# One transfer for x's first two contraction blocks, all TensorE transposes ahead of the first product, and the table load ahead of gate rows

## The chip, the cores and the metric

The kernel runs on one core of a Trainium2 chip. The metric is the device time of one execution in microseconds (us); the times before are 273.25 us in the median of three runs, from 272.84 to 273.96.

## The reference

A feed-forward block with a gated GELU, in bf16, with 1024 tokens (32 x 32), a model width of 1024 and an inner width of 3584:

```python
def reference(x, w_gate, w_up, w_down):
    return (_gelu(x @ w_gate) * (x @ w_up)) @ w_down
```

`x` is (32, 32, 1024), `w_gate` and `w_up` are (1024, 3584), `w_down` is (3584, 1024). `_gelu` is the tanh approximation.

## The kernel before

The tokens are split into two halves of 512 and the contraction of 1024 into eight blocks of 128. The kernel replaces plain 2 x 2 block products by a scheme with fewer products: it forms sums and differences of quarters of the weights (`s1` to `s4`) and of x (`t1` to `t4`) and multiplies those. x is kept transposed, with the contraction on the partitions, in four tiles: `b11` and `b12` hold contraction blocks 0 to 3 for the two token halves, `b21` and `b22` blocks 4 to 7.

The first stage is called ahead in the code. It multiplies the lower half of the gate weights by `b21`, for 24 output tiles in six groups of four (`i` is the group, `j` the tile in it, `k` one of four contraction blocks). The weights of group `i` are in `a12_ahead[i]`, filled by `load_ahead(i, k0, k1)` (L204 to L209); `product_ahead` (L288 to L297) issues the matmuls of some `k` and some columns. This stage starts as soon as the first pieces of x and of the weights have arrived, and this start is all that the change touches.

How the start is arranged, in an order written out by hand (`manual_schedule`):

- The constants and the identity `ident` are made by GpSimd (POOL). TensorE (PE) runs `NWARM` = 6 matmuls on constants (L254), which compute nothing that is used.
- Contraction blocks 4 and 5 of x for the first token half arrive untransposed in `x_nat`, one transfer of 128 KB each: block `dt` = 0 on the queue of SyncE (SP), block `dt` = 1 on the queue of ScalarE (ACT). They are called the first and the second x block below. Each has rows of 256 bytes. Block pieces are transposed by TensorE (L266, four per block), written to PSUM tiles `tps`, and copied to `b21[:, dt]` by VectorE (DVE) in two halves of 256 tokens (L271).
- Contraction blocks 6 and 7 come by a transposing transfer (`load_xT(0, KD + KQ, DT)`, L222) on SP's queue. A tiny GpSimd copy (L221), which reads `x_nat` and writes into the same destination, makes it wait until the first x block has landed.
- Gate weights of groups 0 and 1: SP issues group 0 `k` = 0, group 1 `k` = 0, group 0 `k` = 2 and 3 in one transfer; after the transposing transfer it issues group 1 `k` = 2 and 3. ACT issues, behind a small probe load and the second x block, `k` = 1 of groups 0 and 1. After these five issues, ACT runs a one-column GELU on `ident` (L250 through the helper at L246), ahead of which its table is loaded.
- TensorE's order is: warm matmuls; four transposes of the first x block; `NFILL` = 7 further matmuls on constants, 128 columns each (L275); `by_halves(0)`, that is group 0, `k` = 0, 256 tokens at a time, eight matmuls; four transposes of the second x block; group 1, `k` = 0, for three of four tiles; `by_halves(1)`; the rest of group 1, `k` = 0 and 1; then `k` = 2 and 3 of both groups, each tile copied out when it is complete (L348). Groups 2 to 5 follow.

For the first x block the two token halves have a PSUM tile of their own each; for the second they share one (`whole_tp`). PSUM tiles with the tag A rotate through six banks, so one of group 1's tiles takes over the bank of `whole_tp`; hence its late place in the order.

Of the kernel before, what the change touches and what calls it, by code (L numbers as in the profile page):

```python
# [8 lines left out]
ACT = mybir.ActivationFunctionType  # L9
# [4 lines left out]
def kernel(  # L14
# [20 lines left out]
    nc = tc.nc  # L35
    P = nc.NUM_PARTITIONS
    fp32 = mybir.dt.float32
    f32r = mybir.dt.float32r
    bf16 = mybir.dt.bfloat16
# [3 lines left out]
    xf = x.flatten_outer_dims()  # L43
# [6 lines left out]
    KD = DT // 2  # L50
# [4 lines left out]
    KQ = DT // 4  # L55
    HF = FT // 2
    MT = NB // P
    NWARM = 6
    NFILL = 7
    KB = 4  # L60
    QF = HF // 2
    batches = [(0, KB), (KB, QF), (QF, QF + KB), (QF + KB, HF)]
# [13 lines left out]
    ps1 = ctx.enter_context(tc.tile_pool(name="ps1", bufs=2, space=bass.MemoryType.PSUM))  # L76
# [29 lines left out]
    BANKS = {"A": 6, "C": 2}  # L106

    def acc(tag):
        return ps1.tile([P, NB], fp32, name=f"ps{tag}", tag=tag, bufs=BANKS[tag])
# [3 lines left out]
    a12_ahead = [ring.tile([P, KD, KB * P], bf16, name="a12a", tag="ring") for _ in range(2)]  # L113
    b11 = xpool.tile([P, KD, NB], bf16, name="b11")
    b21 = xpool.tile([P, KD, NB], bf16, name="b21")
# [66 lines left out]
    ones_w = nc.const_aps.tensor(1.0, [P, P], bf16)  # L182
    ones_m = nc.const_aps.tensor(1.0, [P, NB], bf16)
    ident = xpool.tile([P, P], bf16, name="ident")
    make_identity(nc, ident)
    NB_P = NB // P
    probe = xpool.tile([P // 4, KD, 2], bf16, name="probe")
    HALF = NB_P // 2
    x_nat = spool.tile([P, NB_P, KQ * P], bf16, name="x_nat", tag="s1")

    with tc.manual_schedule():
        def load_nat(eng, dt, p0, p1):
            eng.dma_start(
                out=x_nat[:, p0:p1, dt * P : (dt + 1) * P],
                in_=xf[p0 * P : p1 * P, (KD + dt) * P : (KD + dt + 1) * P].rearrange("(b p) d -> p b d", p=P),
            )

        assert KQ == 2
        load_nat(nc.sync, 0, 0, NB_P)


        nc.scalar.dma_start(out=probe, in_=wg_r[::4, KD:, :2])

        def load_ahead(i, k0, k1, eng=nc.sync, j0=0, j1=KB):  # L204
            f0 = i * KB
            eng.dma_start(
                out=a12_ahead[i][:, k0:k1, j0 * P : j1 * P],
                in_=wg_r[:, KD + k0 : KD + k1, (f0 + j0) * P : (f0 + j1) * P],
            )  # L209

        def load_xT(nb, d0, d1):
            t = ((b11, b12), (b21, b22))[d0 // KD][nb]
            nc.sync.dma_start_transpose(
                out=t[:, d0 % KD : (d1 - 1) % KD + 1, :], in_=xf[nb * NB : (nb + 1) * NB, d0 * P : d1 * P]
            )

        load_ahead(0, 0, 1)
        load_nat(nc.scalar, 1, 0, NB_P)
        load_ahead(1, 0, 1)
        load_ahead(0, KQ, KD)  # L220
        nc.gpsimd.tensor_copy(b21[:1, KQ, :1], x_nat[:1, 0, :1])  # L221
        load_xT(0, KD + KQ, DT)  # L222
        load_ahead(0, 1, KQ, nc.scalar)
        load_ahead(1, 1, KQ, nc.scalar)
        a12_ahead += [spool.tile([P, KD, KB * P], bf16, name="a12b", tag=t) for t in ("s2", "s4", "s1", "s3")]
        load_ahead(1, KQ, KD)
        def load_halves(i):
# [16 lines left out]
        def gelu(src, tag, bufs):  # L244
            h = ework.tile([P, NB], bf16, name=tag, tag=tag, bufs=bufs)[:, : src.shape[-1]]
            nc.scalar.activation(h, src, ACT.Gelu_apprx_tanh)  # L246
            return h


        gelu(ident[:, :1], "h0", 6)  # L250

        warm_ps = acc("A")
        for _ in range(NWARM):
            nc.tensor.matmul(warm_ps, lhsT=ones_w, rhs=ones_m, start=True, stop=True)  # L254

        def tp_tile(cols):
            return ps1.tile([P, cols], bf16, name="tp", tag="A", bufs=BANKS["A"])

        tps = [[tp_tile(HALF * P) for _ in range(2)]]
        whole_tp = tp_tile(NB_P * P)  # L260
        tps.append([whole_tp[:, h * HALF * P : (h + 1) * HALF * P] for h in range(2)])

        def transposed(dt):
            for half, tp in enumerate(tps[dt]):
                for b in range(HALF):
                    nc.tensor.transpose(  # L266
                        tp[:, b * P : (b + 1) * P], x_nat[:, half * HALF + b, dt * P : (dt + 1) * P], ident
                    )
            for half, tp in enumerate(tps[dt]):
                p0 = half * HALF * P  # L270
                nc.vector.tensor_copy(b21[:, dt, p0 : p0 + HALF * P], tp)  # L271

        transposed(0)
        for _ in range(NFILL):
            nc.tensor.matmul(warm_ps[:, :P], lhsT=ones_w, rhs=ones_w, start=True, stop=True)  # L275

        def prod(ps, lhs, rhs, start):
            for k in range(KD):
# [9 lines left out]
        def product_ahead(ps, i, j, k0=0, k1=KD, cols=slice(None)):  # L288
            for k in range(k0, k1):
                nc.tensor.matmul(  # L290
                    ps[:, cols],
                    lhsT=a12_ahead[i][:, k, j * P : (j + 1) * P],
                    rhs=b21[:, k, cols],
                    start=(k == 0 and not cols.start),
                    stop=(k == KD - 1),
                    skip_group_check=True,
                )  # L297
# [32 lines left out]

        both = (nc.scalar.copy, nc.vector.tensor_copy)
        ps = [[acc(t) for t in tags] for tags in ("CCAA", "AAAA")]
        def by_halves(k):
            for half in range(2):
                for j in range(KB):
                    product_ahead(ps[0][j], 0, j, k, k + 1, slice(half * HALF * P, (half + 1) * HALF * P))

        by_halves(0)
        transposed(1)
        for j in range(KB - 1):  # L340
            product_ahead(ps[1][j], 1, j, 0, 1)
        by_halves(1)
        for j in range(KB):
            product_ahead(ps[1][j], 1, j, 0 if j == KB - 1 else 1, KQ)
        for i in (0, 1):
            for j in range(KB):
                product_ahead(ps[i][j], i, j, KQ)
# [26 lines left out]
        for ci in range(NCH):  # L374
# [8 lines left out]
            sn5, sn2, h1, h0 = [], [], [], []  # L383
# [17 lines left out]
            if fts[-1] < NAHEAD:  # L401
                h0 = first
# [192 lines left out]
        for h0, h1, upto in ((0, NB - P, NB - P), (NB - P, NB, NB)):  # L595
            cols = slice(h0, h1)
            ps = acc("C")[:, : h1 - h0]
# [33 lines left out]
```

## Time and profile before

| what | value |
|---|---|
| median of the runs | 273.25 us (272.84 to 273.96) |
| the profiled execution | 273.33 us |
| its span, first to last instruction | 271.4 us |
| TensorE busy | 268.0 us, 99% of the span, 1219 matmuls |
| VectorE / ScalarE / GpSimd busy | 75% / 43% / 45% |
| first product matmul starts | 4.46 us into the span |

The profiled time is 1.9 us more than the span; that is what lies around the first and last instruction. A busy TensorE in the profile is not a TensorE at its best pace, and the matmuls' ends are modelled: consecutive matmuls overlap in the record, so the pace is read from the distance between starts. In a timeline row the first number is the start in us, the second the time to the end of the last merged instruction, and `x4` says how many were merged. PE is TensorE's matmuls, PEld its weight loads, SPq and ACTq are instructions that issue transfers from SyncE and ScalarE.

### The profile page before, as it was taken

Reading aid. Unit: us, or ns where it says so; the run is one execution under the profiler, and the core shown is the slowest. Engines: PE = TensorE matmul, PEld = TensorE weight load, DVE = VectorE, ACT = ScalarE, POOL = GpSimd, SP = SyncE. Lnnn points to the kernel's source line nnn. Section 1 sums busy time; section 2 is a strip of 40 time slices with the busy share of each in tenths; the row PEclk is TensorE's granted clock in tenths of the full one; section 3 lists DMA queues with packets and bytes.
Section 4 is the critical chain, followed back from the end, with each engine's and each line's share of the span. In section 5 each row is a group of like instructions: output and inputs, shape, how many; then the busy total and the mean of one; then the engine's idle time right before and its main releaser. Section 6 shows DMA issues by size and latency. Waiting matters only on the chain.

```text
span 271.4 us, 3431 instructions
## 1 busy us (share of the span) xinstructions
PE 268.0 (99%) x1219; PEld 193.7 (71%) x1219; DVE 204.0 (75%) x205; ACT 115.4 (43%) x189; POOL 120.8 (45%) x61
## 2 busy tenths in 40 slices
PE   8999999999999999999999999999999999999996
PEld 5544776886787788688688687764458888888884
DVE  1447999986976877887777478469999999988711
ACT  2435756545644653645636535434000307870000
POOL 1080089997994994995995996000000000000000
PEclk9999999999999999999999999999999999999999
DMA  7999321514505505415234190005981537875111
GB/s 193 316 209 228 100 62 56 157 35 119 157 0 155 156 2 155 126 28 157 73 84 119 47 331 8 0 2 178 356 279 60 156 115 248 269 194 181 52 64 60
DMA packets 56657, 35.88 MB, mean 132 GB/s; under 512 B 10048, under 2 KB 56640, under 8 KB 56640
## 3 DMA queue, kind: packets, MB, share of 16 engines
q1 hardware_dynamic: 53232, 33.17, 43.3%
q10 hardware_dynamic: 3408, 2.49, 2.9%
q8 instruction: 10, 0.16, 0.3%
q14 instruction: 7, 0.06, 0.1%
HBM read 31.72 MB, written 2.10 MB: 125 GB/s over the span
## 4 chain that ended last, share of the span: by engine, by line
PE 99%; DVE 0%; issue 0%
PE psA L279 38%; PE psA L435 24%; PE psC L279 19%; PE psC L435 7%; PE psA L290 5%; PE psC L290 3%; PE psC L599 1%; PE psA L254 1%; PE psA L275 0%; PE tp L266 0%; DVE o_last L600 0%
## 5 line engine op out<-in xcount | busy, mean ns | idle before, releaser
L279 PE MATMUL psA<-t,s 128*128 128x512 f32 x224 | 57.2, 397 | 0.0
L246 ACT ACTIVATE h<-c 128x512 bf16<-128x512 f32 x56 | 34.4, 629 | 41.5 <-DVE c L309 41.5
L279 PEld LDWEIGHTS psA<-t,s 128*128 128x128 f32 x224 | 42.1, 188 | 9.5
L165 POOL TENSOR_TENSOR s<-wu 128x1024 fp32r<-128x1024 bf16 x13 | 29.5, 2271 | 28.0 <-DMA wu<-in_w_up_dram 24.0
L166 POOL TENSOR_TENSOR s<-s,wg 128x1024 fp32r<-128x1024 f32 x14 | 32.0, 2285 | 15.2 <-PE psA L279 14.2
L279 PE MATMUL psA<-b,wg 128*128 128x512 bf16 x128 | 29.4, 380 | 0.0
L168 POOL TENSOR_TENSOR s<-wg,wu 128x1024 fp32r<-128x1024 bf16 x13 | 28.9, 2219 | 0.0
L279 PE MATMUL psA<-t,a22r 128*128 128x512 f32 x112 | 27.9, 391 | 0.0
L279 PE MATMUL psC<-t,s 128*128 128x512 f32 x112 | 27.9, 391 | 0.0
L279 PE MATMUL psC<-b22r,s 128*128 128x512 f32 x112 | 27.7, 389 | 0.0
L309 DVE TENSOR_TENSOR c<-sn,psA 128x512 f32<-128x512 f32 x32 | 21.8, 682 | 6.7 <-PE psA L279 6.1
L314 ACT COPY sn<-psC 128x512 f32<-128x512 f32 x28 | 16.3, 588 | 22.8 <-PE psC L279 14.9
L279 PEld LDWEIGHTS psC<-t,s 128*128 128x128 f32 x112 | 21.0, 188 | 4.5
L279 PEld LDWEIGHTS psA<-t,a22r 128*128 128x128 f32 x112 | 21.0, 188 | 4.5
L279 PEld LDWEIGHTS psC<-b22r,s 128*128 128x128 f32 x112 | 21.0, 188 | 4.4
L309 DVE TENSOR_TENSOR c<-sn,psC 128x512 f32<-128x512 f32 x28 | 19.0, 686 | 6.0 <-PE psC L279 6.0
L412 DVE TENSOR_TENSOR lo<-c,h 128x512 bf16<-128x512 f32 x14 | 22.5, 1605 | 0.9
L279 PEld LDWEIGHTS <-wg 128*128 128x128 bf16 x128 | 11.8, 98 | 15.3 <-issue 2.4
L167 POOL TENSOR_TENSOR s<-wg,s 128x1024 fp32r<-128x1024 bf16 x10 | 21.6, 2160 | 0.8
L314 ACT COPY sn<-psA 128x512 f32<-128x512 f32 x32 | 18.3, 592 | 4.9 <-PE psA L279 4.6
L309 DVE TENSOR_TENSOR c<-ahead,psA 128x512 f32<-128x512 f32 x24 | 16.4, 686 | 3.5 <-PE psA L279 2.1
L412 DVE TENSOR_TENSOR hi<-c,h 128x512 bf16<-128x512 f32 x14 | 17.6, 1257 | 0.9
(88 smaller groups left out, 375.5 us busy)
## 6 DMA issues: line engine op xcount, KB each, us to landing
wu<-in_w_up_dram SPq DMA_DIRECT2D x14, 512.0 KB, 4.1
wdb<-in_w_down_dram SPq DMA_DIRECT2D x12, 512.0 KB, 4.8
wg<-in_w_gate_dram SPq DMA_DIRECT2D x10, 512.0 KB, 5.3
wdb<-in_w_down_dram SPq DMA_DIRECT2D x12, 384.0 KB, 4.5
v<-in_w_down_dram SPq DMA_DIRECT2D x4, 512.0 KB, 6.1
out_dram<-o_sb ACTq DMA_DIRECT2D x15, 128.0 KB, 1.7
v<-in_w_down_dram SPq DMA_DIRECT2D x4, 384.0 KB, 7.5
a12b<-in_w_gate_dram SPq DMA_DIRECT2D x4, 256.0 KB, 4.2
```

What stands on the lines that cost most here:

```text
L165: yield engs[0].tensor_tensor(s1, a21, a22, ADD)
L166: yield engs[1].tensor_tensor(s2, s1, a11, SUB)
L167: yield engs[2].tensor_tensor(s4, a12, s2, SUB)
L168: yield engs[3].tensor_tensor(s3, a11, a21, SUB)
L246: nc.scalar.activation(h, src, ACT.Gelu_apprx_tanh)
L254: nc.tensor.matmul(warm_ps, lhsT=ones_w, rhs=ones_m, start=True, stop=True)
L279: nc.tensor.matmul(ps, lhsT=lhs[:, k, :], rhs=rhs[:, k, :], start=(start and k == 0), stop=(k == KD - 1), skip_group_check=True,)
L290: nc.tensor.matmul(ps[:, cols], lhsT=a12_ahead[i][:, k, j * P : (j + 1) * P], rhs=b21[:, k, cols], start=(k == 0 and not cols.start), stop ...
L309: tt(t, s, ps, ADD)
L314: nc.scalar.copy(t, ps)
L412: tt(g_of(ft)[:, NB:], added(sn5[fl], psa[fl]), h1[fl], MUL)
L435: nc.tensor.matmul(banks[m], lhsT=lhs(k)[:, m * P : (m + 1) * P], rhs=rhs(k), start=(start and k == 0), stop=(k == HF - 1), skip_group_che ...
```

## The change

The two x blocks come in one transfer on SP's queue, with rows of 512 bytes. ACT's queue loses its x transfer; its one-column GELU moves up behind the probe, and now writes into the first column of group 1's `k` = 1 weights, which the transfer issued next overwrites. So ACT issues three gate transfers behind it: group 1 `k` = 1, then group 0 `k` = 2 and `k` = 3 one by one. Group 0 `k` = 1 moves to SP, ahead of the transposing transfer.

On TensorE the fillers become two ahead of the transposes and one behind. All eight transposes stand ahead of the first product, in the order block 0 half 0, block 0 half 1, block 1 half 0, block 1 half 1. The two PSUM tiles are now one per token half, each holding both blocks; four VectorE copies follow in the order of the transposes. The products then run group 0 `k` = 0 by halves, group 1 `k` = 0, group 0 `k` = 1 and group 1 `k` = 1 whole, and from there on as before.

```diff
-        load_nat(nc.sync, 0, 0, NB_P)
+        load_nat(nc.sync, 0, NB_P)
...
         load_ahead(0, 0, 1)
-        load_nat(nc.scalar, 1, 0, NB_P)
         load_ahead(1, 0, 1)
-        load_ahead(0, KQ, KD)
+        load_ahead(0, 1, KQ)
+        nc.scalar.activation(a12_ahead[1][:, 1, :1], ident[:, :1], ACT.Gelu_apprx_tanh)
+        load_ahead(1, 1, KQ, nc.scalar)
+        for k in range(KQ, KD):
+            load_ahead(0, k, k + 1, nc.scalar)
         nc.gpsimd.tensor_copy(b21[:1, KQ, :1], x_nat[:1, 0, :1])
         load_xT(0, KD + KQ, DT)
-        load_ahead(0, 1, KQ, nc.scalar)
-        load_ahead(1, 1, KQ, nc.scalar)
...
-        gelu(ident[:, :1], "h0", 6)
...
-        transposed(0)
-        for _ in range(NFILL):
-            nc.tensor.matmul(warm_ps[:, :P], lhsT=ones_w, rhs=ones_w, start=True, stop=True)
+        tps = [ps1.tile([P, KQ, HALF * P], bf16, name="tp", tag="A", bufs=BANKS["A"]) for _ in range(2)]
...
+        fill(2)
+        for dt in range(KQ):
+            for half in range(2):
+                transposed(half, dt)
+        for dt in range(KQ):
+            for half in range(2):
+                copied(half, dt)
+        fill(1)
...
-        by_halves(0)
-        transposed(1)
-        for j in range(KB - 1):
+        for half in range(2):
+            for j in range(KB):
+                product_ahead(ps[0][j], 0, j, 0, 1, slice(half * HALF * P, (half + 1) * HALF * P))
+        for j in range(KB):
             product_ahead(ps[1][j], 1, j, 0, 1)
-        by_halves(1)
-        for j in range(KB):
-            product_ahead(ps[1][j], 1, j, 0 if j == KB - 1 else 1, KQ)
+        for i in (0, 1):
+            for j in range(KB):
+                product_ahead(ps[i][j], i, j, 1, KQ)
```

More of the change, by code (lines that the diff above doesn't have):

```diff
@@ L58 @@
     NWARM = 6
-    NFILL = 7
     KB = 4
@@ L191, with load_nat @@
     with tc.manual_schedule():
-        def load_nat(eng, dt, p0, p1):
+        def load_nat(eng, p0, p1):
             eng.dma_start(
-                out=x_nat[:, p0:p1, dt * P : (dt + 1) * P],
-                in_=xf[p0 * P : p1 * P, (KD + dt) * P : (KD + dt + 1) * P].rearrange("(b p) d -> p b d", p=P),
+                out=x_nat[:, p0:p1, :],
+                in_=xf[p0 * P : p1 * P, KD * P : (KD + KQ) * P].rearrange("(b p) d -> p b d", p=P),
             )
         assert KQ == 2
-        load_nat(nc.sync, 0, 0, NB_P)
+        load_nat(nc.sync, 0, NB_P)
         nc.scalar.dma_start(out=probe, in_=wg_r[::4, KD:, :2])
@@ L254, with fill, transposed, copied @@
             nc.tensor.matmul(warm_ps, lhsT=ones_w, rhs=ones_m, start=True, stop=True)
[L256 to L271, printed above, removed]
-        transposed(0)
-        for _ in range(NFILL):
-            nc.tensor.matmul(warm_ps[:, :P], lhsT=ones_w, rhs=ones_w, start=True, stop=True)
+        def fill(n):
+            for _ in range(n):
+                nc.tensor.matmul(warm_ps[:, :P], lhsT=ones_w, rhs=ones_w, start=True, stop=True)
+        tps = [ps1.tile([P, KQ, HALF * P], bf16, name="tp", tag="A", bufs=BANKS["A"]) for _ in range(2)]
+        def transposed(half, dt):
+            for b in range(HALF):
+                nc.tensor.transpose(
+                    tps[half][:, dt, b * P : (b + 1) * P],
+                    x_nat[:, half * HALF + b, dt * P : (dt + 1) * P],
+                    ident,
+                )
+        def copied(half, dt):
+            p0 = half * HALF * P
+            nc.vector.tensor_copy(b21[:, dt, p0 : p0 + HALF * P], tps[half][:, dt, :])
+        fill(2)
[6 more added lines that the diff above has]
+        fill(1)
         def prod(ps, lhs, rhs, start):
@@ L332 @@
         ps = [[acc(t) for t in tags] for tags in ("CCAA", "AAAA")]
-        def by_halves(k):
-            for half in range(2):
-                for j in range(KB):
-                    product_ahead(ps[0][j], 0, j, k, k + 1, slice(half * HALF * P, (half + 1) * HALF * P))
-        by_halves(0)
-        transposed(1)
-        for j in range(KB - 1):
+        for half in range(2):
+            for j in range(KB):
+                product_ahead(ps[0][j], 0, j, 0, 1, slice(half * HALF * P, (half + 1) * HALF * P))
+        for j in range(KB):
             product_ahead(ps[1][j], 1, j, 0, 1)
-        by_halves(1)
-        for j in range(KB):
-            product_ahead(ps[1][j], 1, j, 0 if j == KB - 1 else 1, KQ)
+        for i in (0, 1):
+            for j in range(KB):
+                product_ahead(ps[i][j], i, j, 1, KQ)
         for i in (0, 1):
```

## The prediction

> **What bounds the kernel now.** I read first the chain of work that ended last.
>
> ```profile
> PE 99%; DVE 0%; issue 0%
> ```
>
> TensorE is the chain nearly from end to end, so an edit at the start is worth the time by which it moves TensorE's dense run of products, and nothing else. The waits of TensorE and of its weight loads over the first 60 us name one transfer:
>
> ```profile
> PEld L254 <- issue: 1.8, 5, 0.7
> PEld L266 <- DMA x_nat<-in_x_dram: 0.6, 1, 0.6
> PEld L279 <- issue: 0.5, 2, 0.3
> ```
>
> So no product waits there for weights or for x. Then the timeline of the start:
>
> ```profile
> 0.77 2.72 PE L254 MATMUL psA<-const-bfloat16-1.0 128*128 128x512 bf16 x6 [0.77 <-PEq L615]
> ...
> 2.73 1.28 ACT L246 ACT_TABLE_LOAD   x1 [2.73 <-issue]
> 3.23 0.42 PEld L266 LDWEIGHTS <-x_nat 128*128 128x128 bf16 x4 [0.64 <-DMA x_nat<-in_x_dram]
> ...
> 3.28 0.63 PE L266 MATMUL tp<-ident,x_nat 128*128 128x128 bf16 x4
> 3.44 1.34 SPq L213 DMA_TRANSPOSE b<-in_x_dram  x1
> ...
> 3.71 0.95 PE L275 MATMUL psA<-const-bfloat16-1.0 128*128 128x128 bf16 x7
> 3.74 0.50 DVE L271 COPY b<-tp 128x256 bf16<-128x256 bf16 x2 [3.74 <-PE tp L266]
> ...
> 4.35 1.29 PEld L290 LDWEIGHTS <-a12a 128*128 128x128 bf16 x8
> 4.46 0.64 PE L290 MATMUL psC<-b,a12a 128*128 128x256 bf16 x2
> 4.88 0.61 PE L290 MATMUL psA<-b,a12a 128*128 128x256 bf16 x2
> 5.31 0.40 PE L290 MATMUL psC<-b,a12a 128*128 128x256 bf16 x2
> 5.55 0.38 PE L290 MATMUL psA<-b,a12a 128*128 128x256 bf16 x2
> ...
> 5.76 0.39 PE L266 MATMUL tp<-ident,x_nat 128*128 128x128 bf16 x4
> 5.99 0.81 PE L290 MATMUL psA<-b,a12a 128*128 128x512 bf16 x3
> 6.19 0.49 DVE L271 COPY b<-tp 128x256 bf16<-128x256 bf16 x2 [1.94 <-PE tp L266]
> ```
>
> Three things are to be seen. First, the pace: starts of pairs at 4.46, 4.88 and 5.31 are 0.21 us per 256 columns; from 5.31 to 5.55 to 5.76 it is 0.12 and 0.105. TensorE's pace doubles at about 5.34 us. (The granted clock is 1.00 throughout, so it is the starts that show it.) The slow pace is 0.107 us per 128 columns: 4 transposes take 3.28 to 3.71, 7 fillers 3.71 to 4.46. Second, the second block's four transposes cost 0.23 us of the chain, 5.76 to 5.99. Third, the copies. The first x block has one PSUM tile per half, and its first copy starts at 3.74, 0.04 us after its second transpose (3.28 + 0.107 + 0.314 = 3.70). The second has one tile for both halves, and the first copy starts at 6.19, 0.04 us after the end of the fourth (6.15). A copy waits for all transposes into its tile.
>
> Last, two transfers issued together at about 1.2 us, with their times to landing:
>
> ```profile
> x_nat<-in_x_dram ACTq DMA_DIRECT2D x1, 128.0 KB, 3.3
> a12a<-in_w_gate_dram SPq DMA_DIRECT2D x1, 128.0 KB, 3.1
> ```
>
> The weights of the first product land at 1.24 + 3.1 = 4.34 us, and their weight load begins at 4.35. The seven fillers end where those weights arrive. The second x block lands at 1.20 + 3.3 = 4.5, the first at 0.74 + 2.4 = 3.14.
>
> **The change part by part.**
>
> *The one x transfer.* Where the first block's packets are in flight (2.2 to 2.7 us) the rows show 298 GB/s at best, 13.7 ns for a 256-byte packet on each of 16 engines. The chunk loads of 512-byte rows run at 345 GB/s in their steady part, 23.7 ns a packet. The new transfer has the same 512 packets, 32 for each engine, so it ends 32 x 10 ns = 0.32 us later: landing 3.46. Bounds: 3.14 (nothing added) and 4.5, where the second block lands now; I take 3.46, near the first row, because it is alone on the queue ahead of everything but the probe. The Trainium skill, page DMA: Bandwidth & Descriptors, section Specifications, says that line rate needs 512 bytes or more and gives 27 GiB/s for an engine; by that estimate 32 packets take 0.57 us against 0.44 seen for the smaller ones, the landing is 3.27, and the sum below is 0.1 us lower.
>
> *Fillers and transposes.* Warm matmuls end at 3.33, two fillers at 3.54. Now 0.14 us lie between landing and first transpose (3.14 to 3.28), so the transposes start at 3.60 and take 8 x 0.107 = 0.86, to 4.46; one filler to 4.56. The copy of block 0, half 0 now has a tile that also takes block 1, half 0, so it waits for the sixth transpose: 3.60 + 5 x 0.107 + 0.314 = 4.45, starts 4.49, ends 4.77 (0.28 each). With a handoff of 0.05 the first product starts at 4.82, where it is 4.46 now: TensorE idles 0.26 us. The second copy starts 0.25 later and is done at 5.02, before the fifth product; copies three and four are done by 5.52, before group 1 takes those banks (about 5.94). Their cover is those eight products; without it each would add 0.25.
>
> *Sum on TensorE.* Until the pace doubles at 5.34, before did (5.34 - 4.46) / 0.213 = 4.1 matmuls of 256 columns, after does (5.34 - 4.82) / 0.213 = 2.4. The 1.7 lost are made up at 0.108 each: +0.18 us. The four transposes inside the products go: -0.23. Net -0.05. If the pace doubles before the transposes, they take 0.055 each, the first copy ends about 4.4, the first product is as early as now and the gain is -0.2; if it doubles after 6.2, the loss is 0.36 / 2 = 0.18 and the gain 4 x 0.107 = 0.43: -0.25. I take -0.15. Bounds of this part: -0.25, and, with a landing at 4.5, product start 5.86 and (5.86 - 5.34) + 4.1 x 0.108 - 0.23 = +0.73.
>
> *Products reordered.* Group 0, k = 1, is four matmuls of 512 instead of eight of 256: the same columns, four weight loads fewer, and weight loads lie beside matmuls: 0. TensorE's count goes from 1219 to 1211 (four fillers, four halves).
>
> *ScalarE's queue.* Probe issue ends at 1.18; table load 1.28 and activation 0.21 (rows of L246) to 2.7 (identity ready at 1.30, no wait). Queued behind it are three issues of 0.49 us: at 2.75, 3.25, 3.75. With 3.7 to 4.2 us to landing (the rows of gate transfers issued near 2 us) they land at 6.5 to 7.0, 7.0 to 7.5 and 7.5 to 8.0. Needed, counting 0.108 per 256 columns from 5.34: group 1 k = 1 at 7.65, group 0 k = 2 and 3 at 8.5. Cost 0, the cover being 16 matmuls of 512; the margin is 0.5 us at its thinnest. ScalarE's next work is the copy at 9.22.
>
> *SP's and GpSimd's queue.* On SP, group 1 k = 0 keeps its place (1.7), and it and group 0 k = 1 have no ACT transfer beside them until after 2.75, so they land no later than the 5.4 and 5.5 of now; needed at 5.9 and 6.8. GpSimd's copy and the transposing transfer behind it start 0.32 later, 3.76, landing 3.76 + 4.1 = 7.9 (needed 8.5). All that SP issues after is 0.3 late as well: group 1, k = 2 and 3, about 9.4 (needed 10.3); the later transposing transfers delay t1 and t2, and t2 ends at 28.25 for a product at 29.44: 0.3 fits in 1.2. Cost 0 now; without that cover, 0.3.
>
> Sum: 273.33 - 0.15 = 273.2 against the profiled execution, which lies 0.08 above the median; I forecast **273.1 us**, within 0.5% of before, which is about what a measurement of this kernel can tell from no change.
>
> **Rivals.**
>
> *The pace doubles later (slower).* The slow pace ran from 0.77 to 5.34, 4.57 us of near-dense matmuls, and 0.43 us of transposes stood in it. After the change 0.86 of transposes and 0.26 of idle time stand there. If that is too thin and the count of 4.57 starts again with the first product, the doubling moves from 5.34 to 4.82 + 4.57 = 9.39. It decides if some 1.1 us without product or filler is too much where 0.43 was not. Price: half of 4.05, +2.0: **275.2**. For it: no row shows the pace doubling sooner. Against: 0.43 us of transposes did not hinder it, and transposes ran at the fast pace after it (0.055 apart from 5.76). The Trainium skill, page TensorE: Matmul & The Clock Gate, Part 4, says that transposes do not count as busy work for the clock, and Part 1 gives a free-running window of 3.4 us; by these the doubling would slip one window and the estimate is +1.7, 274.9. The trace does not decide whether transposes count.
>
> *The x transfer lands late.* At 4.5, as the second block does now: +0.73, **274.0**. For it: 256 KB are then behind one semaphore. Against: what made the second block late now is that it shared the engines with the first weights.
>
> *A gate or x row lands late.* ACT's third gate transfer or the transposing transfer lands 0.5 past its need at 8.5: **273.6 to 274.0**. Against: the margins above.
>
> *The change doesn't hold copies back.* If a copy waits only for its own two transposes, the first product follows the filler at 4.56 and the sum is -0.2: **273.0**.
>
> **How the numbers follow.** Forecast 0.60, its own range 272.6 to 273.7, from the bounds of the TensorE part and the spread of the runs before (272.84 to 273.96, which a shift of the doubling by 2 us would give). Later doubling 0.14, late x 0.09, late gate row 0.09, copies not held 0.08. Faster by 0.5% would be under 271.9: no case reaches it, 0.05 for what I don't see. Slower by 0.5% is above 274.6: the later doubling and a little of the late rows, 0.16. The range of 8 in 10 reaches from 272.3 over late x and late rows to 274.5, and leaves the later doubling out.
>
> **What would show it.** Right: one x transfer landing near 3.46, first transposes at 3.6, the first copy after the sixth transpose, first product near 4.8, no transposes among products, pairs 0.21 apart until about 5.3, 1211 matmuls, no wait of a product for a transfer. Wrong: starts 0.21 apart beyond 6 us, a weight load that waits for gate rows near 8 us, or a first transpose after 4.

## The result and the profile after

The changed kernel takes 274.39 us in the median (273.95 to 275.18), the kernel before beside it 273.18 (272.80 to 273.96). The ratio is 1.0041, with a 95% interval of 1.0029 to 1.0052: 1.2 us slower, where I had forecast 0.15 faster. The time lies inside the range that I had put at 8 in 10 (272.3 to 274.5); the direction is wrong. The profiled execution, at 273.95 us with a span of 272.0, is the fastest of them, so its trace shows only part of the loss: 0.62 us against the 273.33 of before's profiled execution.

The chain of work that ended last is no longer TensorE alone. Its shares of the changed kernel, by engine and by line:

```profile
PE 96%; DMA 3%; issue 0%; DVE 0%; POOL 0%
PE psA L283 38%; PE psA L435 24%; PE psC L283 19%; PE psC L435 7%; PE psA L294 4%; PE psC L294 2%; DMA b<-in_x_dram 2%; PE psC L599 1%; DMA x_nat<-in_x_dram 1%; DVE o_last L600 0%; POOL b L223 0%
```

The transposing transfer, GpSimd's copy and the x transfer that releases it now stand in the chain. The same chain in order of time, its first 15 us (start, length, what):

```profile
0.74 2.90 DMA x_nat<-in_x_dram
3.63 0.05 issue
3.69 0.19 POOL b L223
3.87 0.02 issue
3.89 4.76 DMA b<-in_x_dram
8.65 0.14 issue
8.78 1.13 PE psC L294 x4
```

The timeline of the changed kernel's start, to be held against the one shown in the prediction:

```profile
1.21 1.28 ACT L219 ACT_TABLE_LOAD   x1 [1.21 <-PEq L615]
...
2.50 0.20 ACT L219 ACTIVATE a12a<-ident 128x1 bf16<-128x1 bf16 x1
2.74 2.90 ACTq L205 DMA_DIRECT2D a12a<-in_w_gate_dram  x3
...
3.68 1.00 PE L262 MATMUL tp<-ident,x_nat 128*128 128x128 bf16 x8
...
4.54 0.88 DVE L270 COPY b<-tp 128x256 bf16<-128x256 bf16 x4 [4.54 <-PE tp L262]
4.88 0.38 PE L294 MATMUL psC<-b,a12a 128*128 128x256 bf16 x2
...
8.78 1.13 PE L294 MATMUL psC<-b,a12a 128*128 128x512 bf16 x4 [0.28 <-DMA b<-in_x_dram]
9.09 2.92 PEld L294 LDWEIGHTS <-a12a 128*128 128x128 bf16 x15 [0.24 <-DMA a12a<-in_w_gate_dram]
...
12.34 1.89 PE L294 MATMUL psC<-b,a12b 128*128 128x512 bf16 x8
```

Two rows of the kernel before that stand against these, ScalarE's gate transfers and group 2:

```profile
1.69 1.01 ACTq L206 DMA_DIRECT2D a12a<-in_w_gate_dram  x2
...
12.04 1.89 PE L290 MATMUL psC<-b,a12b 128*128 128x512 bf16 x8
```

TensorE did its part as predicted and somewhat faster, because the pace had doubled before the first product at 4.88. The products of k = 0 and 1 are issued by 8.35. Then k = 2 waits for the transposing transfer, which lands at 8.65, and k = 3 for a gate row, which lands at 9.04. Group 2 starts at 12.34, where it was 12.04. Before, no product waited for a transfer here.

ScalarE's row shows the step that I had mis-sized: three issues take 2.90 us, where I had reckoned with three of 0.49. Taken one by one, the second and third in the changed kernel:

```profile
3.65 0.33 ACTq L205 DMA_DIRECT2D a12a<-in_w_gate_dram  x1
5.26 0.38 ACTq L205 DMA_DIRECT2D a12a<-in_w_gate_dram  x1
```

The trace names the semaphore that each transfer completes on: the mark that tells that it has landed. SP and ScalarE share eight of them, taken in turn. The turn is not the order of the code, where ScalarE's three issues stand sixth to eighth: by the semaphores that they carry, behind the table load they have the eighth, tenth and twelfth turn, with SP's transfers between them. The second issue takes over the semaphore of the x transfer, which lands at 3.63, and the third that of group 1, k = 0, which lands at 5.24. Each is issued 0.02 us after the earlier user has landed. In the kernel before, exactly eight transfers stand ahead of the transposing one, and ScalarE issues its last at 2.24 without a wait.

A second, smaller step lies at 41 us. These rows of the timeline answer each other. The kernel before:

```profile
25.96 2.29 DVE L361 TENSOR_TENSOR t<-b,t 128x2048 fp32r<-128x2048 bf16 x1 [0.94 <-DMA b<-in_x_dram]
...
40.31 1.98 PE L279 MATMUL psA<-t,a22r 128*128 128x512 f32 x8
42.12 1.98 PE L279 MATMUL psC<-b22r,s 128*128 128x512 f32 x8
```

The changed kernel, same view:

```profile
26.88 2.29 DVE L361 TENSOR_TENSOR t<-b,t 128x2048 fp32r<-128x2048 bf16 x1 [1.56 <-DMA b<-in_x_dram]
...
40.58 2.19 PE L283 MATMUL psA<-t,a22r 128*128 128x512 f32 x8
42.61 1.99 PE L283 MATMUL psC<-b22r,s 128*128 128x512 f32 x8
```

The lag grows from 0.27 to 0.49 us: SP's queue runs late, the transposing transfer for t2 lands 0.9 later, VectorE's chain behind it is 0.9 later, and TensorE then waits 0.4 for one of its additions (line L313). From there to the last instruction the lag stays at 0.5; the other 0.1 of the 0.62 lies outside the span.

### The profile page after: what moved, and what is told of

The parts are those of the page before. It is cut to its first block, busy times and chain, and to the rows that moved or that the text cites. A ratio compares the mean times of both kernels' runs of the same rounds, so it can differ in the third digit from the quotient of the medians.

```text
span 272.0 us, 3401 instructions
## 1 busy us (share of the span) xinstructions
PE 267.3 (98%) x1198; PEld 192.6 (71%) x1211; DVE 200.9 (74%) x205; ACT 115.6 (43%) x189; POOL 120.2 (44%) x61
## 4 chain that ended last, share of the span: by engine, by line
PE 96%; DMA 3%; issue 0%; DVE 0%; POOL 0%
PE psA L283 38%; PE psA L435 24%; PE psC L283 19%; PE psC L435 7%; PE psA L294 4%; PE psC L294 2%; DMA b<-in_x_dram 2%; PE psC L599 1%; DMA x_nat<-in_x_dram 1%; DVE o_last L600 0%; POOL b L223 0%
## 5 line engine op out<-in xcount | busy, mean ns | idle before, releaser
L165 POOL TENSOR_TENSOR s<-s,wg 128x1024 fp32r<-128x1024 f32 x14 | 31.3, 2236 | 15.5 <-DVE s L164 14.5
L283 PE MATMUL psA<-b,wg 128*128 128x512 bf16 x119 | 27.8, 379 | 0.6
L313 DVE TENSOR_TENSOR c<-sn,psA 128x512 f32<-128x512 f32 x32 | 21.8, 682 | 6.7 <-PE psA L283 5.7
L313 DVE TENSOR_TENSOR c<-sn,psC 128x512 f32<-128x512 f32 x28 | 19.1, 687 | 6.0 <-PE psC L283 6.0
L412 DVE TENSOR_TENSOR lo<-c,h 128x512 bf16<-128x512 f32 x14 | 20.6, 1471 | 0.9
L313 DVE TENSOR_TENSOR c<-ahead,psA 128x512 f32<-128x512 f32 x24 | 16.4, 686 | 3.5 <-PE psA L283 2.3
L331 DVE TENSOR_TENSOR hi<-h,psA 128x512 bf16<-128x512 bf16 x14 | 9.6, 688 | 12.4 <-PE psA L283 12.4
```

Source lines behind the costliest of these rows:

```text
L165: yield engs[1].tensor_tensor(s2, s1, a11, SUB)
L283: nc.tensor.matmul(ps, lhsT=lhs[:, k, :], rhs=rhs[:, k, :], start=(start and k == 0), stop=(k == KD - 1), skip_group_check=True,)
L313: tt(t, s, ps, ADD)
L331: tt(g_of(ft)[:, :NB], h0, psa, MUL)
L412: tt(g_of(ft)[:, NB:], added(sn5[fl], psa[fl]), h1[fl], MUL)
```

## The experiments

Times are medians; each ratio is against the kernel before on the same chip, with its 95% interval. Where a time of the pace's doubling is given, it is read from the starts of TensorE's rows, as in the prediction.

**The changed kernel again.** Two further profiles, no edit.

> The changed kernel once more, for a second profile. Theory X (the transposing transfer of x's blocks 6 and 7 lands at 8.65 us, after the products of k = 0 and 1 are done at 8.35, and TensorE waits): the start of k = 2 is again later than before's 8.6 us, at 8.8 or more, with the wait on that transfer shown, and the time is 1.0 to 1.4 us over before. Theory P (the pace doubles later in most executions than in the one profiled): products 0.21 us apart beyond 5.4 us, and no wait on the transfer.

> The changed kernel a third time, beside the two variants that follow. Theory S (ScalarE's second and third gate transfers are held back before their issue by waits for the completion of the x transfer and of group 1's k = 0 row, whose completion semaphores they take over): the third is issued at 5.2 to 5.6 us again, within 0.05 us of the landing of that row, lands at 8.9 to 9.5, and the product of k = 3 waits for it. Time 0.4 to 1.3 us over before. Theory D (the transfers are late because the engines that move them are shared): the third issue is not tied to that landing.

after_again: 273.97 us, 1.0025 (1.0010 to 1.0039). after_third: 274.13, 1.0030 (1.0016 to 1.0044). The third ScalarE issue came at 5.40 and 5.63, 0.02 us after group 1, k = 0, had landed at 5.38 and 5.61, and its row landed at 9.21 and 10.16. The wait on it in after_again:

```profile
8.28 0.38 PE L294 MATMUL psC<-b,a12a 128*128 128x512 bf16 x1
9.26 0.82 PE L294 MATMUL psC<-b,a12a 128*128 128x512 bf16 x3 [0.60 <-DMA a12a<-in_w_gate_dram]
```

One product of k = 2 runs, and the next, of k = 3, starts 0.98 later, where 0.22 is its pace. So theory X named the wrong transfer for this execution: the transposing one had landed at 7.79. In all three profiles of the changed kernel the held-back gate row is late. The pace doubled near 4.6, at 4.2 and at 6.5.

**Gate transfers and table load.** First the old places for both, in the changed kernel:

```diff
-        load_ahead(0, 1, KQ)
-        nc.scalar.activation(a12_ahead[1][:, 1, :1], ident[:, :1], ACT.Gelu_apprx_tanh)
-        load_ahead(1, 1, KQ, nc.scalar)
-        for k in range(KQ, KD):
-            load_ahead(0, k, k + 1, nc.scalar)
+        load_ahead(0, KQ, KD)
+        load_ahead(0, 1, KQ, nc.scalar)
+        load_ahead(1, 1, KQ, nc.scalar)
```

(and the one-column GELU back in front of the warm matmuls).

> The changed kernel with the gate transfers and the table load put back as before: the one x transfer and TensorE's new order stay. Theory X with the gate rows as the cause (ScalarE's late gate transfers share the engines with the transposing transfer and stretch it from 4.1 to 4.8 us): the transfer takes 4.1 to 4.3 us again, lands near 8.1, the wait is gone, and 0.5 to 1.2 us of the loss return (273.2 to 273.9). Theory X with the issue as the cause (the transfer is issued 0.45 us later because the x transfer lands later): it still lands after 8.4 and the loss stays, 274.2 to 274.6. Theory P: no difference, 274.4.

273.83 us, 1.0019 (1.0008 to 1.0030). The transposing transfer, issued at 3.92, took 3.55 us and landed at 7.47; no product waited. But only 0.14 us came back against after_again on the same chip, less than its uncertainty.

Then the reverse: the new gate order in the kernel before (the removed lines above, put behind the second x block).

> The kernel before with only the gate transfers and the table load moved as in the change (behind the second x block on ScalarE's queue). Gate rows as the cause: the transposing transfer, issued at 3.44, takes 4.7 to 5 us instead of 4.1 and lands at 8.1 to 8.5, close to its need at 8.6, and ScalarE's third gate row, issued some 0.5 us later than in the change, lands at 8.5 to 9: a wait of up to 0.4 us, time 273.2 to 273.8. Issue as the cause, or theory P: as before, 273.2.

274.53 us, 1.0045 (1.0028 to 1.0062). This one edit costs 1.1 us, more than any theory gave. ScalarE's second issue waited for the second x block (landed 4.41, issued 4.43); the third followed at 4.81, when its own semaphore was just free (group 1, k = 0, had landed at 4.75). The two rows landed at 8.87 and 9.62. Behind the table load the first issue came at 3.31; with 0.35 us for an issue, the others would have come near 3.7 and 4.0 without the semaphores, an estimate. So the semaphores held these rows back by some 0.8 us each, and the rest of their delay is the table load's. The waits of TensorE over the first 14 us:

```profile
PE psA L254 <- PEq L615: 0.8, 1, 0.8
PE psC L290 <- DMA a12a<-in_w_gate_dram: 1.1, 2, 0.7
```

The transposing transfer landed at 6.92, earlier than in the kernel before, so it is the gate rows that were late. To keep all the change but the holding back, ScalarE's three issues were put ahead of the table load:

```diff
         load_ahead(0, 1, KQ)
-        nc.scalar.activation(a12_ahead[1][:, 1, :1], ident[:, :1], ACT.Gelu_apprx_tanh)
         load_ahead(1, 1, KQ, nc.scalar)
...
+        gelu(ident[:, :1], "h0", 6)
+
         warm_ps = acc("A")
```

> The changed kernel with one thing moved: ScalarE issues its three gate transfers ahead of the table load. The same transfers on the same queues, but now the first eight transfers are all issued before any semaphore is taken over. Theory S: ScalarE issues at 1.2, 1.7 and 2.2 us without a wait, the k = 2 and 3 rows land by 6.6, no product waits for a gate row, and the time is 0.3 to 0.9 us below the changed kernel of this call, 0 to 0.4 over before (what is left is the later first product, near 4.9). Theory D: the rows land no earlier than 8.5, since the same bytes share the same engines, and the time is that of the changed kernel.

273.95 us, 1.0024 (1.0008 to 1.0039). In its profile ScalarE's three issues are one unbroken row, the last row landed at 7.01 (10.16 in after_third), and the only wait of a product for a gate row, 0.05 us, was for SP's group 0, k = 1:

```profile
1.22 1.50 ACTq L205 DMA_DIRECT2D a12a<-in_w_gate_dram  x3
2.75 1.28 ACT L245 ACT_TABLE_LOAD   x1 [2.75 <-issue]
```

The profiled execution took 273.38 us, span 271.5. So theory S holds for the rows, against D: the same bytes on the same engines, 2 to 3 us earlier. It does not hold for the median, which fell by 0.18 us where 0.3 or more was expected. Something else was left, and the times, 273.38 to 275.65, were wide.

The two held rows in one transfer, behind the table load (`load_ahead(0, KQ, KD, nc.scalar)` for the loop over k):

> The changed kernel with the k = 2 and 3 gate rows in one transfer, behind the table load as in the change: ScalarE issues two instead of three, and the second waits for the x transfer's completion alone. Theory S: it is issued at 3.65 to 3.75, lands at 7.3 to 8.2, and the waits of k = 3 go; 0.2 to 0.8 us below the changed kernel. The table load as such as the cause: no gain, since the table load stands where it stood.

274.46 us, 1.0033 (1.0022 to 1.0045): no gain. Issued at 3.76 after the x transfer's 3.74, it landed at 8.10, as expected; but the transposing transfer now landed at 9.06 and the wait of 0.6 moved to that.

**SP's wait for x.** GpSimd's tiny copy reads the identity instead of `x_nat`:

```diff
-        nc.gpsimd.tensor_copy(b21[:1, KQ, :1], x_nat[:1, 0, :1])
+        nc.gpsimd.tensor_copy(b21[:1, KQ, :1], ident[:1, :1])
```

> The changed kernel with GpSimd's tiny copy reading the identity instead of x: the transposing transfer no longer waits for the x transfer and is issued at about 2.7 instead of 3.89 us. Theory X: it lands by 7.5 to 8.0, the wait at 8.5 is gone, and 0.5 us or more of the 1.2 return (273.2 to 273.9). Theory P: no difference, 274.4. If sharing the engines with the gate rows is what counts, they land later by as much and the wait moves to them: 274 to 274.4.

275.01 us, 1.0065 (1.0041 to 1.0089), slower still. The transposing transfer was issued at 2.73, 1.16 earlier than in the changed kernel, and landed at 7.84, 0.8 earlier. The third gate row was issued at 5.55 and landed at 10.47, after 4.9 us instead of 3.8, and TensorE waited 2.0 us for it. The wait moved to the gate rows, as the last theory had it.

**What is left with the gate rows ahead.** All of these are after_late_table with one more edit, or with none:

> The changed kernel with the gate transfers ahead of the table load once more, beside the two above and for a second profile. Its times reached from 273.38 to 275.65. Theory T: with the profile's time above 273.9, one of the transfers (x, the transposing one, a gate row) lands later than in the first profile (3.65, 7.88, 7.01) and a product waits for it; with it near 273.4, none does. Theory P (the pace doubles later): the starts stay 0.21 us apart per 256 columns beyond 6 us in a slow profile.

> The changed kernel with the gate transfers ahead of the table load a third time, as the one to compare the two above with: 0.4 to 0.6 over before in the median, the transposing transfer issued at 3.9 to 4.1.

274.05 us, 1.0017 (1.0006 to 1.0028), and 274.17, 1.0034 (1.0012 to 1.0055). Both profiles show the first product at 4.95 to 5.02 and the pace doubling at 6.4, where the profile at 273.38 us had 4.90 and 5.25. Both also show t2 starting 1.2 to 1.7 us later than before and products waiting near 41 us.

A PSUM tile for each half of each block, so that the first copy waits for two transposes:

```diff
-        tps = [ps1.tile([P, KQ, HALF * P], bf16, name="tp", tag="A", bufs=BANKS["A"]) for _ in range(2)]
+        tps = [[ps1.tile([P, HALF * P], bf16, name="tp", tag="A", bufs=BANKS["A"]) for _ in range(KQ)] for _ in range(2)]
```

> The changed kernel with the gate transfers ahead of the table load, and one PSUM tile for each half of each x block, so that the first copy waits for the second transpose and no longer for the sixth. Theory C (what is left of the loss, 0.5 us in the median, is the later first product): the first copy starts near 4.2 instead of 4.55, the first product at 4.55 to 4.65 instead of 4.9, and the time is 0.15 to 0.35 below the run with the gate transfers alone moved. Theory T (what is left is transfers that land late in some executions): no difference in the median.

274.61 us, 1.0039 (1.0024 to 1.0053). The first product did start earlier, at 4.79 although x landed at 3.81, and it didn't help: theory C falls. The pace doubled at 6.5.

TensorE's old order with the new transfers (one x transfer, gate rows ahead of the table load; `NFILL` = 3):

> One x transfer and the gate transfers ahead of the table load, but TensorE's order, PSUM tiles and halves of the kernel before, with three fillers behind the first four transposes. Theory O (TensorE's new order is what costs): the first product at 4.5, time that of before, 273.2 to 273.5. Theory T (the one x transfer and what it delays is what costs, whatever TensorE's order): 273.8 to 274.1, as the changed kernel with the gate transfers ahead of the table load.

274.06 us, 1.0023 (1.0011 to 1.0034): the same loss. So TensorE's new order is not what costs, and theory O falls. x landed at 3.92; TensorE waited for it with no filler ahead, and the pace doubled near 6.8.

SP freed of its wait for x, now without a held-back gate row:

> The changed kernel with the gate transfers ahead of the table load, and GpSimd's tiny copy reading the identity, so that SP no longer waits for the x transfer but only for the probe's (landing near 3.3). Theory Q (what is left of the loss is SP's queue running 0.5 us later from the transposing transfer on, which grows down the queue): the transposing transfer is issued near 3.35, the big transposing transfer behind it near 10.6 to 11.0, the transfer that t2 waits for lands by 26.0, and the time is 0 to 0.25 over before, 0.3 below the run with SP waiting. Theory F (what is left is the first product at 4.9): no difference, 0.45 to 0.6 over before.

274.30 us, 1.0035 (1.0020 to 1.0051): no gain. The transposing transfer was issued at 3.74, but the big one behind it only at 11.70 and t2's landed at 27.39, so the edit did not bring SP's later queue back, and theory Q was not really put to the test there. x landed at 3.96, the first product started at 5.21, the pace doubled at 6.4.

Two x transfers, one behind the other on SP (and k = 2 and 3 in one gate transfer):

```diff
-        load_nat(nc.sync, 0, NB_P)
+        load_nat(nc.sync, 0, 0, NB_P)
+        load_nat(nc.sync, 1, 0, NB_P)
```

> The same start, but the two x blocks in two transfers, one behind the other on SP, and the k = 2 and 3 gate rows in one, so that eight transfers stand ahead of the transposing one again. That one now waits for the first x block alone. Theory Q: issued near 3.5, and 0 to 0.25 over before. Theory F: the first product still waits for the second block and starts at 4.9 to 5.0; 0.45 to 0.6 over before.

275.78 us, 1.0087 (1.0074 to 1.0100), worse than either theory. The second block landed at 4.92. TensorE idled from 3.9 to 4.97 and from 5.5 to 6.15, and the pace doubled only at 9.4:

```profile
3.50 0.63 PE L263 MATMUL tp<-ident,x_nat 128*128 128x128 bf16 x4
4.97 0.61 PE L263 MATMUL tp<-ident,x_nat 128*128 128x128 bf16 x4 [0.84 <-DMA x_nat<-in_x_dram]
5.37 0.31 PE L257 MATMUL psA<-const-bfloat16-1.0 128*128 128x128 bf16 x1
6.15 0.61 PE L295 MATMUL psC<-b,a12a 128*128 128x256 bf16 x2 [0.47 <-DVE b L271]
...
7.40 2.19 PE L295 MATMUL psA<-b,a12a 128*128 128x256 bf16 x6
9.43 0.59 PE L295 MATMUL psC<-b,a12a 128*128 128x512 bf16 x2
9.86 1.46 PE L295 MATMUL psA<-b,a12a 128*128 128x512 bf16 x6
```

From 9.43 to 9.86 two matmuls of 512 columns are 0.215 each; the ones before them were 0.43. That pointed at the rival which I had given 0.14: idle time that holds the pace down.

**Idle time and the pace.** Only the fillers of the kernel before are changed: none (`NFILL` = 0), or seven transposes of the identity in their place.

```diff
-            nc.tensor.matmul(warm_ps[:, :P], lhsT=ones_w, rhs=ones_w, start=True, stop=True)
+            nc.tensor.transpose(fill_tp, ident, ident)
```

> The kernel before without its seven fillers: TensorE idles from 3.71 to the landing of the first product's weights, near 4.35, and starts the first product when it did. Nothing else moves. Theory P (idle time and transposes in the first microseconds make the pace double later): the profile or the median shows it; starts 0.21 us apart beyond 6 us, and 0.2 to 0.6 over before. If the pace does not depend on it: as before, within 0.15.

> The kernel before with the seven fillers replaced by seven transposes of the identity, which take the same time and are read by nothing. If transposes do not count as work for the pace, as the Trainium skill's page on TensorE says (TensorE: Matmul & The Clock Gate, Part 4): like the run without fillers, 0.2 to 0.6 over before if theory P holds. If they count: as before, within 0.15.

Without fillers: 274.12 us, 1.0025 (1.0002 to 1.0047), times from 272.68 to 275.43. With transposes: 273.53, 1.0003 (0.9987 to 1.0019), times from 272.94 to 274.25. The starts without fillers:

```profile
3.29 0.63 PE L266 MATMUL tp<-ident,x_nat 128*128 128x128 bf16 x4
4.64 0.61 PE L290 MATMUL psC<-b,a12a 128*128 128x256 bf16 x2 [0.73 <-DMA a12a<-in_w_gate_dram]
...
8.03 0.61 PE L290 MATMUL psC<-b,a12a 128*128 128x256 bf16 x2
8.46 0.41 PE L290 MATMUL psA<-b,a12a 128*128 128x256 bf16 x2
8.70 0.38 PE L290 MATMUL psC<-b,a12a 128*128 128x256 bf16 x2
```

The pace is slow up to 8.46. With seven transposes instead it was fast from 4.5 on in the profile. In these two profiles, one of each, the idle time did harm and the transposes did not. The medians say less. Three of the twelve executions without fillers have 3.0 to 3.8 us outside the span, where no execution of the kernel before has more than 2.1; what that time is, the runs do not show. By the span the medians are 271.8 without fillers and 271.5 before, which their spread does not tell apart.

The converse, in after_late_table: fillers until x lands and until the first copy is done.

```diff
-        fill(2)
+        fill(5)
...
-        fill(1)
+        fill(4)
```

> The changed kernel with the gate transfers ahead of the table load and more fillers: five ahead of the transposes and four behind, so that TensorE has no idle time up to the first product, which starts near 5.1 instead of 4.9. Theory P: the pace doubles by 6.0 as in the kernel before and the time is 0 to 0.25 over before, against 0.45 to 0.8 without the fillers. Theory T (transfers that land late in some executions are what is left): 0.5 to 0.9 over before, since the first product is 0.2 later still.

273.67 us, 1.0008 (0.9992 to 1.0024), times from 273.28 to 274.13. The first product starts 0.15 to 0.25 later than without these fillers, at 5.16, and yet most of the loss in the times is gone, and with it their upper end (275.65, 274.70 and 276.52 in the three runs without). The interval still overlaps theirs, and by the span 0.3 us of the loss are left against 0.40 to 0.55, so the gain is not certain. The pace doubled at 5.8, within the range of the profiles without these fillers (5.25 to 6.4), so this run does not show that the pace is what they mended. Its starts, without a gap of more than 0.1 us:

```profile
3.29 0.74 PE L257 MATMUL psA<-const-bfloat16-1.0 128*128 128x128 bf16 x5
3.90 1.03 PE L263 MATMUL tp<-ident,x_nat 128*128 128x128 bf16 x8
4.73 0.63 PE L257 MATMUL psA<-const-bfloat16-1.0 128*128 128x128 bf16 x4
5.16 0.64 PE L295 MATMUL psC<-b,a12a 128*128 128x256 bf16 x2
```

**The kernel before once more, and a version to beat it.**

> The kernel before once more, for a second profile of it. In six profiles of other variants the pace of TensorE doubled at 3.7 to 6.5 us. Expected: first product at 4.35 to 4.5, no product waits for a transfer, whenever the pace doubles; time 272.7 to 274.0, the lower the earlier it doubles, by half a microsecond for each.

273.45 us, 1.0002 (0.9989 to 1.0015). The pace doubled at 4.5 and no product waited for a transfer at the start; the profiled time was 273.05, against 273.33 where it doubled at 5.34. That is 0.28 us for 0.84 us, less than the half that I had put. At the start the half does hold: ScalarE's first copy of a finished tile came 0.37 us earlier (8.85 against 9.22), and 0.1 of it was lost near 41 us.

The version keeps the kernel before and takes from the change that ScalarE's rows should not run beside the first weights:

```diff
-        load_ahead(0, KQ, KD)
+        load_ahead(0, 1, KQ)
+        load_ahead(1, 1, KQ, nc.scalar)
+        load_ahead(0, KQ, KD, nc.scalar)
...
-    NFILL = 7
+    NFILL = 5
```

(the two later ScalarE issues of k = 1 are dropped).

> The kernel before with group 0 k = 1 issued by SP and group 1 k = 1 and group 0 k = 2 and 3 by ScalarE, all eight first transfers without a taken-over semaphore and ahead of the table load, and five fillers instead of seven. In the run of the kernel before with the new gate order the weights of the first product landed at 3.94 instead of 4.30, because no ScalarE gate row ran beside them. Theory S: they land at 4.0 to 4.3, the first product starts at 4.25 instead of 4.46, nothing waits later, and the time is 0 to 0.3 us below before. Theory D: ScalarE's 256 KB beside the first rows keeps them at 4.3 or later, and the time is that of before.

273.42 us, 0.9995 (0.9985 to 1.0006). The first weights landed at 4.01 and the first product started at 4.24, 0.22 earlier; the time is that of before. In its profile the pace doubled at 6.4, so an earlier start ran at the slow pace.

## Why the prediction was wrong

*TensorE's own part held in its order of events.* The first copy waited for the sixth transpose (4.54, forecast 4.49), the first product started at 4.88 (4.82), the products of k = 0 and 1 waited for nothing, and the transposes among them went. The times agree partly by luck: x landed 0.17 late, but the transposes followed it by 0.05 us where I had put 0.14. The gain of 0.15 is not seen: in after_late_table, whose pace doubled about when before's did, ScalarE's first copy of a finished tile came only 0.06 us earlier (9.16 against 9.22). one_x_old_order against after_late_table shows no difference from the order.

*The x transfer landed later than its row said.* Forecast 3.46; it landed at 3.63 to 3.96 in the profiles with one transfer ahead of everything on SP, 0.45 to 0.8 after the first block of before instead of 0.32. The size was off, within the bounds of 3.14 to 4.5.

*"Queued behind it are three issues of 0.49 us: at 2.75, 3.25, 3.75" is the first step that failed.* They came at 2.74, 3.65 and 5.26. I had counted the instructions that ScalarE issues, but not the completion semaphores they need. With the table load ahead, two of them no longer fall among the first eight transfers and wait for an earlier user's landing; the third would have been issued near 3.45 without that (an estimate, from issues of 0.35 behind the first at 2.74). The last row landed at 9.04 to 10.16, where 8.0 was the latest I had allowed. That the semaphores hold the issues back is shown: by the 0.02 us between landing and issue in all three profiles, and by its absence when the issues go ahead of the table load. That late gate rows cost time is shown by before_new_gate at 1.0045, where TensorE waited for nothing else from the first product to 14 us, though there the table load delays them as well. What the rows cost in the changed kernel's median is not shown: with them on time it fell by 0.18 us only.

*The transposing transfer.* Issued at 3.89 (3.76) and landed between 7.8 and 8.65 in the changed kernel's profiles (forecast 7.9). Its need at 8.5 came earlier where the pace doubled early: the products were through at 8.35. A TensorE that gets faster at the start runs into its transfers; the kernel before, with all of them in time, keeps what it gains.

*The rival with the later doubling, priced at 0.14, is seen at work in two variants, but in no profile of the changed kernel.* The record of the granted clock (last section) says when the pace doubles: at the end of a stretch of 3.41 us, on a grid that each execution finds somewhere else, and only of a stretch with little idle time. So the doubling falls anywhere from 3.5 to 6.8 us by luck, and enough idle time puts it off by one stretch. That happened without fillers and with two x transfers (8.5 and 9.3 us). With one x transfer it happened in none of the eleven profiles that have the record: in each, the last stretch after which the clock did not go up had begun before TensorE's first matmul, and the 0.77 us ahead of that matmul alone made it as idle as the one without fillers. So idle time is not shown to be a cause of the changed kernel's loss. The price of half a microsecond for each by which the pace doubles later was right: in the three profiles of after_late_table and its repeats it doubled at 5.2, 6.4 and 6.4, and ScalarE's first copy came 0.06 us earlier than before's, 0.55 later and 0.49 later. What the rival had wrong was to add up transposes and idle time. The Trainium skill (TensorE: Matmul & The Clock Gate, Part 4, PE-mode transpose) says that transposes do not count as work for the clock gate; in before_tp_fill the clock went up after a stretch with 1.0 us of transposes, and in before_no_fill not after one with 0.73 us without any matmul (by the ends that the profile models). That speaks against it here, and the measurement decides; the trace calls these transposes MATMUL and does not tell their mode. Its Part 1 says that the window is free-running and that the slow stretch varies from run to run; that agrees with doublings between 3.5 and 6.8 us in profiles with the same warm matmuls. So a single profile can't price it: the one of after doubled near 4.6, and its execution was the fastest of all.

*"0.3 fits in 1.2" failed too.* In the changed kernel's three profiles VectorE's work on t2 started not 0.3 but 0.6 to 2.6 us late; each of SP's issues waits in turn for an earlier landing. By how far TensorE's lag behind the kernel before grows between 14 and 60 us, it cost 0.2 us in the first profile of the changed kernel, nothing in after_again, 0.75 in after_third and 0.3 to 0.7 in four of the variants.

The causes hide each other. A product that waits for its gate row at 9 us doesn't care whether it came there at the slow pace; with the gate rows alone mended the median moved by less than its uncertainty, and with more fillers as well it came to 1.0008. What the fillers would do with the gate rows still held back was not tried. How much each is worth in the changed kernel's median can't be given apart. In the profiles with the gate rows on time, what is left beside the luck of the doubling is the lateness of SP's queue; that it explains the medians is not shown, and theory Q stays open.

## What to carry to other kernels

Before a transfer is moved behind something slow, count the transfers in flight, in the order in which they get their semaphores: with the eight of this kernel, the ninth is issued when the first user of its semaphore has landed, and everything behind it on that engine waits as well. Keep TensorE busy, with anything, until its first products: 0.9 us of idle time ahead of the first product went with a doubling 3 us later in one profile, and with 0.7 us in the median of the times but only 0.3 in that of the spans; filler transposes were as good as filler matmuls. A start that differs from run to run needs its profile taken several times before a term is sized from it.

## What the runs showed that I had not expected

The time at which TensorE's pace doubles, from the starts in each profile (dense: no idle time up to the first product beyond some 0.1 us):

| start | pace doubles at (us) |
|---|---|
| dense: before, before_again, before_new_gate, before_sp_first, before_tp_fill, late_table_dense | 5.3, 4.5, 4.3, 6.4, 4.5, 5.8 |
| one x transfer, 0.4 to 0.8 us idle (twelve profiles) | 3.7 to 6.8, six of them near 6.4 or later |
| idle 0.9 us or more in one piece: before_no_fill, late_table_split_x | 8.5, 9.4 |

The first two rows cover the same range. The granted clock in the profile's rows is 1.00 through all of this, but these rows are means. The trace's own record of the clock, kept in 19 of the 20 traces, has its first entry, 1.00, within 0.2 us of the doubling read from the starts (5.33 in the kernel before) and nothing ahead of it; an entry of 0.50 follows at the end of the execution. So what doubles is the granted clock, and a mean of 1.00 only says that the slow time has no entry.

The entries at 1.00 last 266.24 us in fourteen of the traces and 269.65 in five. The two differ by 3.41 us and are 78 and 79 times that, whatever the kernel, so the clock changes on a grid of 3.41 us. By the ends that the profile models for matmuls, the stretch of the grid that ends at the doubling has at most 0.65 us without a matmul in all 19, and the one before it at least 0.73. Where the grid lies differs from execution to execution. At half the price, 3.41 us are worth 1.7; the times of the kernel before, from 272.66 to 274.29 with one more at 275.62, spread about as far, though nothing shows that the grid is what spreads them.

And the 256 KB of x, first on its queue with nothing but the probe ahead, landed anywhere from 3.63 to 3.96 us when issued at 0.74.
